# Trading an output quarter with two filter units in the batch plan, and ending on ScalarE's stores alone

## The chip, the core and the metric

The kernel runs on one core of one Trainium2 chip. TensorE (PE in the profile) multiplies, VectorE (DVE) and ScalarE (ACT) work on its results, GpSimd (POOL) and SyncE (SP) mostly start transfers; ACT can start them too. The metric is the device time of one execution in microseconds (us). A lower time is better.

## The reference

Two independent branches are computed from two inputs of shape 2048 x 448 and written side by side.

```python
q = (x @ wq).reshape(B, S, H, Dh).transpose(0, 2, 1, 3)   # H = 16 heads of Dh = 28
k = x @ wk                                                # one key and one value head for all
v = x @ wv
p = softmax(einsum("bhqd,bkd->bhqk", q, k) * Dh ** -0.5)
a = einsum("bhqk,bkd->bhqd", p, v).transpose(0, 2, 1, 3).reshape(B, S, H * Dh) @ wo
X = rfft2(B_x, axes=(-2, -1)) * (w_r + 1j * w_i)          # S x (D//2+1) spectrum
b = irfft2(X, s=(S, D), axes=(-2, -1))
out = concatenate([a, b], axis=-1)
```

## The kernel before

**Start.** Queries, keys and values are projected on TensorE, and the first stage of the Fourier filter runs beside that.

**Middle.** The attention is cut into 256 steps. A step is one of 16 blocks of 128 keys, against one chunk `c` of 512 rows and one group `g` of four heads; step number = 16 * (4c + g) + key block. Each step has four score products (line 917, 128x512, one per head), four exponentials on ACT (line 852, or a copy by DVE on line 923 and a later exponential in place, line 942), and then 16 products with the values (line 863). Results of products lie in eight PSUM banks (`s0` to `s5`, `sx`, `po`), and a score product needs a bank that ACT or DVE has emptied.

Steps go in batches. A table `PLAN` has one string for each batch, written out by `spread(n, units, ...)`: `n` steps, whose scores come first (`-`: exponential by ACT at once; `k`: copied by DVE first), with units of other work set between them; after the scores come the products with the values of the whole batch. I count batches from 0 by their place in `PLAN`. The letters are:

- `X` stands for four `W`s, `wo_unit(c, k, 0..3)`: the output projection of one block `k` of 128 rows of chunk `c`, over all four groups (11 products on line 771), then a copy by DVE and a store. I call an `X` an output quarter, since four make a chunk.
- `Z` is one filter unit of the last Fourier stage. For each of eight pieces `q` there are four: `fft3_a(q, 0)`, `fft3_a(q, 1)` (line 675), `fft3_b(q, 0)`, `fft3_b(q, 1)` (lines 699 to 701). `ZZ` is two units.

Which quarter or which unit comes at a letter is only the next in its list, so the letters' order decides it. Loads that a unit needs (`c2` on SP, line 666, and `fi` on POOL, line 668) are placed by the step of their first unit; the queues of SP, POOL, ACT, DVE and PE each work in order.

A finished pair (c, g) is divided by its sums on DVE, split into a coarse part `oh` and a rest `ol`, and then `spares(c, g)` copies rows of `ol` into unused rows of `oh` (SP, line 732, four transfers) and of `ol` (POOL, line 735, four transfers). An output quarter of chunk `c` reads them for every `g`.

**End.** The last chunk's projection is not in the plan. Behind the last products with the values, for its four row blocks k = 0 to 3, `partial(k)` multiplies the first three groups (nine products) and `final(k)` the last group (three products, lines 968 to 970) and stores the block with `wo_out`. The stored tile `yb` has two buffers: blocks 0 and 2 share one, and blocks 1 and 3 share the other, so the copy of block 3 waits until block 1's store has landed.

After that each engine reads a word `bits` (line 994) and branches on it (line 995). The branch leads past a large exact version of the attention, which these inputs don't take. SP then waits for the semaphores of all transfers, and a barrier of all engines ends the program (line 1181, which stands for the program's end).

Of the kernel before, what the change touches and what calls it, by code (L numbers as in the profile page):

```python
# [14 lines left out]
AF = mybir.ActivationFunctionType  # L15
# [5 lines left out]
S, D, H = 2048, 448, 16  # L21
# [16 lines left out]
def spread(n, units, lazy=4, start=0.9, rest=0.85, apart=1.0):  # L38

    late = 8 if lazy > 4 else 4  # L40
    m = 4 * n - late
    out = [(float(i), "-") for i in range(m)]
    out += [(apart * j + 0.5 if j < lazy else m + 0.1 * j, "k" if j < lazy else "e") for j in range(late)]
    out += [(m * (j + start) / (len(units) + rest) - 0.4, u) for j, u in enumerate(units)]
    return "".join(k for _, k in sorted(out)).replace("X", "WWWW").replace("Y", "ZZ")


PLAN = ["eeee"] + ["eeeeF"] + [spread(2, "", 0, 1.05)] + 2 * [spread(2, "", 0)] + [spread(5, "A", 4, 1.6)]
# [10 lines left out]
PLAN += [spread(7, "X", 8, 0.6, 0.35, 1.5)] + [spread(7, "ZZZ", 8, 0.9, 0.6, 1.5)]  # L59
PLAN += [spread(7, "Z", 8, 0.45, 0.6, 2.0)] + [spread(7, "ZZZ", 8, 0.9, 0.97, 2.5)]  # L60
PLAN += [spread(7, "ZZZ", 8, 0.9, 0.6, 2.0)] + [spread(8, "ZZZ", 7, 0.9, 0.6, 2.0)]
PLAN += [spread(7, "X", 8, 0.6, 0.6, 2.0)] + [spread(6, "X", 8, 0.9, 0.6, 2.0)]
PLAN += [spread(7, "ZZ", 8, 0.9, 0.6, 1.75)] + [spread(7, "X", 8, 0.9, 0.6, 2.25)]
PLAN += [spread(7, "X", 8, 0.6, 0.6, 1.5)] + [spread(7, "ZZZ", 8, 0.6, 0.6, 2.0)]
PLAN += [spread(7, "ZZ", 8, 0.9, 0.6, 2.0)] + [spread(7, "ZZ", 8, 0.6, 0.85, 2.0)]

# [5 lines left out]
def kernel(ctx: ExitStack, tc: tile.TileContext, t: dict):  # L72
    nc = tc.nc
# [73 lines left out]
    def fft1_a_mm(q, p):  # L147
        f, cs1 = ff[q], fc["cs1"][:113]
        pa = pair_of(bank())
        for e in range(2):  # L150
            for k, (n, o0) in enumerate(((113, 0), (112, 113))):
                for h in range(2):
                    for r in range(2):
                        r0 = 64 * h + 32 * r
                        mm(pa[r0:r0 + 32, e, o0:o0 + n], f[:, 2 * r + k, 2 * p + e, h], cs1[:, 2 * r + k, :n],  # L155
                           start=True, stop=True)
        return pa

    def fft1_a_out(q, p, pa):
        a = at1[q, p] = fp.tile([128, 2, DF], F32, name="a", tag=("pwr", "pwi")[p])  # L160
        return nc.scalar.activation(a, pa, AF.Copy)

    def fft1_b(q):
        return fft1_out(q, fft1_mm(q))
# [92 lines left out]
    with tc.tile_pool(name="w1", bufs=1) as w1:  # L257
# [37 lines left out]
        with tc.tile_pool(name="x1", bufs=2) as x1:  # L295
# [63 lines left out]
            def evac(c, g, pq):  # L359
                cs = slice(c * CW, (c + 1) * CW)  # L360
                out = nc.scalar.activation(qraw[:, g, cs], pq, AF.Copy)
                nc.vector.tensor_reduce(qmx[:, g, c:c + 1], qraw[:, g, cs], axis=AX.X, op=ALU.max,
                                        apply_absolute_value=True)
                return out
# [55 lines left out]
            for c in range(1, NC):  # L420
                for g in range(NG):
# [3 lines left out]
                    last = evac(c, g, pq)  # L425
# [43 lines left out]
        for p in range(2):  # L469
            last = fft1_a_out(6, p, fft1_a_mm(6, p))  # L470
# [7 lines left out]
        last = fft1_b(5)  # L478
# [26 lines left out]
    d, f, a, b, e, c = free  # L505
# [6 lines left out]
    def take():  # L512
        ready, bank = free.pop(free.index(min(free, key=lambda x: x[0])))
        clock["pe"] = max(clock["pe"], ready + 100)
        return bank
# [32 lines left out]
    def at_once(work=640, engine="dve"):  # L548
        clock[engine] = max(clock[engine], clock["pe"] + 200) + work
# [215 lines left out]
    def wo_mm(p, c, k, gs):  # L765
        s = slice(k * 128, k * 128 + 128)
        for g in gs:
            for n, (x, w) in enumerate(((oh, woh[:, g]), (ol, wox[:, g - 1] if g else woh[:, 0]), (oh, wol[:, g]))):
                if n == 1 and g == 0 and c < NC - 1:
                    continue  # L770
                mm(p, x[c][:, g, s], w, start=(g == 0 and n == 0), stop=(g == NG - 1 and n == 2))  # L771

    def wo_out(p, c, k, last=0):
        y = pp.tile([128, D], F32, name="yb", tag=f"p{k % 2}") if last else ap.tile([128, D], F32, name="ya")
        r0 = c * CW + k * 128
        for e in ((0, 1) if last == 4 else (0,)):
            s = slice(e * D // 2, (e + 1) * D // 2) if last == 4 else slice(0, D)
            if last and not e:
                nc.scalar.activation(y[:, s], p[:, s], AF.Copy)
            else:  # L780
                nc.vector.tensor_copy(y[:, s], p[:, s])
                at_once()
            (nc.scalar if last == 4 and not e else nc.sync).dma_start(t["oa"][r0:r0 + 128, s], y[:, s])

    wps = {}

    def wo_unit(c, k, g):
        if g == 0:
            wps[c, k] = take()
        p = wps[c, k][:, :D]  # L790
        need(("o", c, g))
        for x in (g,) if g == 0 else (g, g + NG - 1):
            need(("wo", x))
        wo_mm(p, c, k, (g,))
        passed(600 if g else 400)
        if g == NG - 1:
            wo_out(p, c, k)
            give(wps.pop((c, k)))
# [95 lines left out]
    for tokens in PLAN:  # L894
# [10 lines left out]
        for k in tokens:  # L905
# [9 lines left out]
            c, g, kc = steps[i if kind == "-" else n - 1 - i]  # L915
# [21 lines left out]
        for i in reversed(range(stay)):  # L937
# [5 lines left out]
            else:  # L943
                for h in hs:
                    p = keep[i][h // 2][:, h % 2]
# [12 lines left out]
    c = NC - 1  # L958
    ws = []

    def partial(k):
        ws.append(take()[:, :D])
        wo_mm(ws[k], c, k, range(NG - 1))

    def final(k):
        p, s = ws[k], slice(128 * k, 128 * k + 128)
        h, l = oh[c][:, NG - 1, s], ol[c][:, NG - 1, s]
        mm(p, h, woh[:, NG - 1], start=False, stop=False)
        mm(p, l, wox[:, NG - 2], start=False, stop=False)
        mm(p, h, wol[:, NG - 1], start=False, stop=True)  # L970
        wo_out(p, c, k, k + 1)


    flush(kept)
# [1 line left out]
    for k in range(4):  # L976
        divide(c, NG - 1, k)
        s = slice(128 * k, 128 * k + 128)
# [3 lines left out]
        nc.vector.tensor_tensor(ol[c][:, NG - 1, s], on[:, s], h.bitcast(F32), op=ALU.subtract)  # L982
    for k in (0, 1):
        partial(k)
    for k in (2, 3):
        final(k - 2)
        partial(k)
    final(2)
    final(3)


# [3 lines left out]
    with tc.If(rv > int(np.float32(BOUND).view(np.int32))), tc.tile_pool(name="g1", bufs=1) as g1:  # L995
# [32 lines left out]
        oa = t["oa"].rearrange("(n p) d -> n p d", p=128)  # L1028
        with tc.For_i(0, NC, 1) as nq:
            y = g1.tile([128, 4, D], F32, name="y")  # L1030
            nc.vector.memset(y, 0.0)
            with tc.For_i(0, NG, 1) as ng:
# [5 lines left out]
                for i in range(4):  # L1038
# [3 lines left out]
                    with tc.For_i(0, 16, 1) as nk:  # L1042
# [5 lines left out]
                        p = g1.tile([128, CW], F32, name="pe")  # L1048
# [136 lines left out]
```

## Time and profile before

| | |
|---|---|
| median of 3 runs | 640.84 us (639.79 to 642.42) |
| profiled execution | 640.64 us, its span 638.9 us |
| busy: PE, ACT, DVE, POOL | 628.8, 547.0, 440.8, 61.1 us |
| granted TensorE clock | 0.997 of full speed |
| batch 38 (steps 201 to 207) | from 500.65 to 518.03 us of the span |
| batch 39 (steps 208 to 213) | 518.03 to 531.26 |
| batch 40 (steps 214 to 220) | 531.26 to 546.01 |
| last products with values end, end stage begins | 621.79 |

The span goes from the first to the last instruction of the program; 1.74 us of the profiled execution lie outside it. Positions in the text are us from the span's start. "PE busy" is no measure of speed, since products overlap in the pipeline; how far apart the starts of products lie is one.

### The profile page before, as it was taken

What the parts mean: (1) busy time and instruction counts of PE and PEld (TensorE: products, weight loads), DVE (VectorE), ACT (ScalarE), POOL (GpSimd) and SP (SyncE); (2) the same over time, 40 slices, a digit from 0 to 9 for tenths busy, and PEclk for the clock granted to TensorE, in tenths of its full rate; (3) what the DMA queues carried; (4) which work ended last, traced back from release to release, by engine and by line L of the source; (5) the groups of instructions that cost most, each with busy time, mean ns of one, the idle gap of its engine ahead of it and who ended that gap; (6) DMA issues with size and microseconds to landing.
All of it is one profiled execution on the core that took longest, in us unless ns stands there. A gap on an engine that the chain in (4) does not pass through costs nothing.

```text
span 638.9 us, 12167 instructions
## 1 busy us (share of the span) xinstructions
PE 628.8 (98%) x4442; PEld 378.3 (59%) x4442; DVE 440.8 (69%) x793; ACT 547.0 (86%) x983; POOL 61.1 (10%) x118
## 2 busy tenths in 40 slices
PE   9999999999999999999999999999999899999995
PEld 7877645656555556646555665555556555555554
DVE  5999648889998934856766845386687446476652
ACT  5654999999999998988999989899989799889881
POOL 3021401011202110001110100001010100000000
PEclk9999999999999999999999999999999999999998
DMA  8855963456454613125340503044331404120011
GB/s 276 267 167 154 263 177 87 114 145 184 114 158 114 154 48 82 60 71 178 83 114 9 136 16 81 15 103 127 80 87 38 120 18 109 39 69 30 2 30 61
DMA packets 37459, 66.74 MB, mean 104 GB/s; under 512 B 7961, under 2 KB 21930, under 8 KB 36428
## 3 DMA queue, kind: packets, MB, share of 16 engines
q1 hardware_dynamic: 32608, 53.31, 30.1%
q0 software_dynamic: 4640, 12.48, 7.5%
q8 instruction: 36, 0.59, 0.4%
q14 instruction: 31, 0.25, 0.1%
q10 hardware_dynamic: 144, 0.11, 0.1%
HBM read 29.81 MB, written 17.87 MB: 75 GB/s over the span
## 4 chain that ended last, share of the span: by engine, by line
PE 96%; DMA 1%; SPq 1%; DVE 0%; issue 0%; ACT 0%; ACTq 0%; DVEq 0%
PE s L863 30%; PE s L917 28%; PE s L357 6%; PE sx L917 5%; PE po L917 5%; PE po L863 4%; PE s L771 4%; PE s L155 2%; PE sx L771 1%; PE s L675 1%; PE pbb L174 1%; PE s L572 1%; PE s L573 1%; PE s L574 1%; PE sx L675 1%; PE s L305 1%
## 5 line engine op out<-in xcount | busy, mean ns | idle before, releaser
L852 ACT ACTIVATE p<-s 128x512 f32<-128x512 f32 x410 | 223.7, 637 | 28.7 <-PE s L917 28.0
L917 PE MATMUL s<-qa,ka 128*128 128x512 f32 x751 | 226.6, 403 | 0.0
L917 PEld LDWEIGHTS s<-qa,ka 128*128 128x128 f32 x751 | 137.2, 188 | 62.1 <-issue 27.7
L863 PE MATMUL s<-p,vs 128*32 128x512 f32 x1040 | 129.7, 595 | 0.0
L923 DVE COPY k<-s 128x512 f32<-128x512 f32 x116 | 76.4, 685 | 56.8 <-PE s L917 56.5
L852 ACT ACTIVATE qraw<-s 128x512 f32<-128x512 f32 x138 | 79.2, 654 | 5.0 <-PE s L917 4.9
L942 ACT ACTIVATE k<-k 128x1024 f32<-128x1024 f32 x80 | 83.5, 1143 | 0.0
L863 PEld LDWEIGHTS s<-p,vs 128*32 128x32 f32 x1040 | 31.4, 109 | 68.5 <-issue 63.3
L917 PE MATMUL sx<-qa,ka 128*128 128x512 f32 x143 | 57.4, 401 | 0.0
L863 PE MATMUL s<-qraw,vs 128*32 128x512 f32 x432 | 55.4, 593 | 0.0
L917 PE MATMUL po<-qa,ka 128*128 128x512 f32 x130 | 52.6, 405 | 0.0
L852 ACT ACTIVATE p<-po 128x512 f32<-128x512 f32 x74 | 47.1, 637 | 4.5 <-PE po L917 4.2
L852 ACT ACTIVATE p<-sx 128x512 f32<-128x512 f32 x60 | 38.6, 644 | 3.9 <-PE sx L917 3.8
L863 PE MATMUL s<-k,vs 128*32 128x512 f32 x320 | 41.8, 594 | 0.0
L735 POOL DMA_DIRECT2D ol<-ol x36 | 18.0, 508 | 230.5 <-DVE ol L758 153.3
L917 PEld LDWEIGHTS sx<-qa,ka 128*128 128x128 f32 x143 | 26.9, 188 | 10.3 <-issue 4.2
L863 PEld LDWEIGHTS s<-qraw,vs 128*32 128x32 f32 x432 | 13.5, 110 | 30.8 <-issue 29.0
L867 DVE STREAM_TRANSPOSE osb<-s 128x512 f32<-128x512 f32 x14 | 10.0, 716 | 31.2 <-PE s L863 31.1
L917 PEld LDWEIGHTS po<-qa,ka 128*128 128x128 f32 x130 | 24.4, 188 | 10.8 <-issue 5.0
L923 DVE COPY k<-sx 128x512 f32<-128x512 f32 x27 | 18.5, 684 | 13.0 <-PE sx L917 13.0
L923 DVE COPY k<-po 128x512 f32<-128x512 f32 x17 | 11.6, 685 | 21.5 <-PE po L917 21.4
L852 ACT ACTIVATE qraw<-sx 128x512 f32<-128x512 f32 x34 | 21.8, 640 | 2.6 <-PE sx L917 2.6
(280 smaller groups left out, 964.8 us busy)
## 6 DMA issues: line engine op xcount, KB each, us to landing
qa<-qa SPq DMA_DIRECT2D x15, 512.0 KB
raw<-xa SPq DMA_DIRECT2D x16, 256.0 KB
xb<-xb SPq DMA_DIRECT2D x8, 512.0 KB
qa<-qh SPq DMA_DIRECT2D x64, 64.0 KB
qa<-ql SPq DMA_DIRECT2D x60, 64.0 KB
t<-bs SPq DMA_DIRECT2D x16, 225.0 KB
wr<-wr POOLq DMA_DIRECT2D x16, 225.0 KB, 3.9
wi<-wi POOLq DMA_DIRECT2D x16, 225.0 KB, 5.3
```

The costliest lines, as they stand in the source:

```text
L155: mm(pa[r0:r0 + 32, e, o0:o0 + n], f[:, 2 * r + k, 2 * p + e, h], cs1[:, 2 * r + k, :n], start=True, stop=True)
L174: mm(pb[h][64 * e:64 * e + 64, p], w[64 * h:64 * h + 64, 2 * p + e], a[64 * h:64 * h + 64, e], start=True, stop=True)
L357: mm(pq, w[:, j, gs], x[:, j], start=(j == 0 and n == 0), stop=(j == 3 and n == 1))
L675: mm(pz[:w, j], c2["c", q][:, j, o0:o0 + w], c2["F", q][:, j], start=True, stop=True)
L735: nc.gpsimd.dma_start(ol[c][o, g].bitcast(F32), ol[c][r, 0].bitcast(F32))
L771: mm(p, x[c][:, g, s], w, start=(g == 0 and n == 0), stop=(g == NG - 1 and n == 2))
L852: nc.scalar.activation(tiles[-1][:, h % 2], sc, AF.Exp, scale=SCALE)
L863: mm(po[c, g][32 * i:32 * i + 32], vs[:, kc], ps[i // 2][:, i % 2], start=(n == 1), stop=(n == 16))
L867: nc.vector.transpose(o, po[c, g])
L917: begun.append(mm(sc, ka[:, kc * 128:(kc + 1) * 128], qa[c, g][:, h], start=True, stop=True))
L923: nc.vector.tensor_copy(keep[i][h // 2][:, h % 2], sc)
L942: nc.scalar.activation(p, p, AF.Exp, scale=SCALE)
```

## The change

There are three edits. In `PLAN`, batch 38 had an output quarter and batch 40 two filter units; they trade places (the pacing numbers go with them). In `wo_out`, block 3 of the last chunk was cut in two halves, one copied and stored by ACT and the other copied by DVE and stored by SP, and blocks 0 to 2 were copied by ACT and stored by SP; now all four are copied whole by ACT, and stored by ACT. In the end stage, `partial(3)` came ahead of `final(2)` and now comes behind it.

```diff
-PLAN += [spread(7, "X", 8, 0.6, 0.6, 2.0)] + [spread(6, "X", 8, 0.9, 0.6, 2.0)]
-PLAN += [spread(7, "ZZ", 8, 0.9, 0.6, 1.75)] + [spread(7, "X", 8, 0.9, 0.6, 2.25)]
+PLAN += [spread(7, "ZZ", 8, 0.9, 0.6, 1.75)] + [spread(6, "X", 8, 0.9, 0.6, 2.0)]
+PLAN += [spread(7, "X", 8, 0.6, 0.6, 2.0)] + [spread(7, "X", 8, 0.9, 0.6, 2.25)]
...
-    def wo_out(p, c, k, last=0):
+    def wo_out(p, c, k, last=False):
...
-        for e in ((0, 1) if last == 4 else (0,)):
-            s = slice(e * D // 2, (e + 1) * D // 2) if last == 4 else slice(0, D)
-            if last and not e:
-                nc.scalar.activation(y[:, s], p[:, s], AF.Copy)
-            else:
-                nc.vector.tensor_copy(y[:, s], p[:, s])
-                at_once()
-            (nc.scalar if last == 4 and not e else nc.sync).dma_start(t["oa"][r0:r0 + 128, s], y[:, s])
+        if last:
+            nc.scalar.activation(y, p, AF.Copy)
+        else:
+            nc.vector.tensor_copy(y, p)
+            at_once()
+        (nc.scalar if last else nc.sync).dma_start(t["oa"][r0:r0 + 128], y)
...
-        wo_out(p, c, k, k + 1)
+        wo_out(p, c, k, True)
...
-    for k in (2, 3):
-        final(k - 2)
-        partial(k)
+    final(0)
+    partial(2)
+    final(1)
     final(2)
+    partial(3)
     final(3)
```

Line numbers behind `wo_out` fall by two in the changed kernel (917 becomes 915, 994 becomes 993, and so on).

On PE, in the middle of batch 38's scores, there stand before (`s4` is a bank, `woh`, `wol`, `wox` are parts of the output weights, `qa` queries, `ka` keys):

```order
L917 MATMUL s5_90<-qa_4457,ka_67 128x512
L917 MATMUL s3_88<-qa_4457,ka_67 128x512
L771 MATMUL s4_89<-woh_1059,oh_4144 128x448
L771 MATMUL s4_89<-wol_1060,oh_4144 128x448
L771 MATMUL s4_89<-woh_1059,oh_4144 128x448
L771 MATMUL s4_89<-wox_1061,ol_4145 128x448
```

In the changed kernel, at the same place on PE, with `c2` and `zh` the data of piece q = 5:

```order
L915 MATMUL s5_90<-qa_4457,ka_67 128x512
L699 MATMUL s3_88<-c2_4626,cs3h_3122 113x256
L700 MATMUL s3_88<-c2_4626,cs3l_3123 113x256
L701 MATMUL s3_88<-zl_4802,cs3h_3122 113x256
L699 MATMUL s3_88<-zh_4774,cs3h_3122 113x256
```

The quarter that read `oh` and `ol` here now begins in batch 39, and the unit `fft3_b(5, 1)` stands in its place; `fft3_a(6, 0)` follows 12 scores later.

On SP, from the last four copies of `oh` on, in the order before (`qa_5043` are the queries of step 224 and on):

```order
L732 DMA oh_4144<-ol_4145 4x512 x3
L230 DMA qa_4762<-qa_4762 64x2048
L732 DMA oh_4144<-ol_4145 4x512
L783 DMA oa<-ya_4941 128x448
L228 DMA qa_5043<-qh_5041 32x512
```

And in the changed kernel, on SP from the same copies on, where `qa_5054` are those queries:

```order
L732 DMA oh_4144<-ol_4145 4x512 x3
L230 DMA qa_4762<-qa_4762 64x2048
L732 DMA oh_4144<-ol_4145 4x512
L666 DMA c2_5501<-t2_73 32x4x225 x3
L720 DMA ob<-yo_4946 112x512
L715 DMA ob<-y1_4941 112x512
L716 DMA oc<-y1_4941 1x512
L666 DMA c2_5501<-t2_73 32x4x225
L228 DMA qa_5054<-qh_5052 32x512
```

The load of `c2` for piece 7 and the stores of piece 5's results now stand ahead of those queries' copies.

SP's end before, from the last store of the filter on:

```order
L716 DMA oc<-y1_5779 1x512
L783 DMA oa<-yb_5891 128x448
L783 DMA oa<-yb_5906 128x448
L783 DMA oa<-yb_5921 128x448
L783 DMA oa<-yb_5927 128x224
L994 TENSOR_LOAD bits_70
L995 COMPARE_AND_BRANCH
```

SP's end in the changed kernel:

```order
L720 DMA ob<-yo_5784 112x512
L715 DMA ob<-y1_5779 112x512
L716 DMA oc<-y1_5779 1x512
L993 TENSOR_LOAD bits_70
L994 COMPARE_AND_BRANCH
```

SP's four stores are gone, so that its word and its branch follow the filter's last store; on ACT the four copies now alternate with four stores, ahead of ACT's own word and branch.

## The prediction

> **What bounds the kernel now.** I began with the page's busy times and its chain of work that ended last.
>
> ```profile
> span 638.9 us, 12167 instructions
> PE 628.8 (98%) x4442; PEld 378.3 (59%) x4442; DVE 440.8 (69%) x793; ACT 547.0 (86%) x983; POOL 61.1 (10%) x118
> PE 96%; DMA 1%; SPq 1%; DVE 0%; issue 0%; ACT 0%; ACTq 0%; DVEq 0%
> ```
>
> TensorE sets the time nearly everywhere, so only what makes PE stand, or what comes behind its last product, can be won. The view of waits, for PE alone, has two rows; this is the one that lies in the middle, and the chain names its transfer:
>
> ```profile
> PE s L771 <- DMA oh<-ol: 1.8, 1, 1.8
> 502.30 4.72 DMA oh<-ol
> ```
>
> The timeline shows the place, first PE, then SP, which issues the transfer:
>
> ```profile
> 504.94 0.37 PE L771 MATMUL s<-wol,oh 128*128 128x448 f32 x1
> 507.16 0.45 PE L771 MATMUL s<-woh,oh 128*128 128x448 f32 x1 [1.84 <-DMA oh<-ol]
> 499.64 1.92 SPq L732 DMA_DIRECT2D oh<-ol  x3
> 502.30 0.59 SPq L732 DMA_DIRECT2D oh<-ol  x1
> ```
>
> This is batch 38. Its output quarter is chunk 2's first and needs the last pair's rows in `oh`; the fourth transfer is issued at 502.3 and lands 4.7 later, while PE already stands in front of the quarter's last three products. The next product should have started 0.2 after 504.94 and starts 2.2 after, so PE loses 2.0.
>
> Behind PE's last product there are 7 us more. The timeline gives PE's end and ACT's copies, the view by line the branch and what follows it, and SP's waits name the longest standstill there (the duration columns are minimum/median/maximum in ns, then first and last start):
>
> ```profile
> 631.40 0.36 PE L970 MATMUL po<-wol,oh 128*128 128x448 f32 x1
> 631.24 0.55 ACT L779 ACTIVATE yb<-s 128x448 f32<-128x448 f32 x1 [1.87 <-PE s L970]
> 632.34 0.36 ACT L779 ACTIVATE yb<-po 128x224 f32<-128x224 f32 x1 [0.56 <-DMA oa<-yb]
> 632.73 0.39 DVE yb L781
> L783 SPq DMA_DIRECT2D oa<-yb x4: 333/342/350, 627.0 to 633.2; - x4
> L994 SPq TENSOR_LOAD <-bits x1: 495/495/495, 633.5 to 633.5; - x1
> L995 SPq COMPARE_BRANCH  x1: 50/50/50, 634.1 to 634.1; - x1
> SPq L995 <- SPq L995: 2.6, 1, 2.6
> L995 SPq EVENT_SEMAPHORE  x6: 17/17/17, 636.8 to 637.2; - x6
> L1181 SPq EVENT_SEMAPHORE  x14: 17/28/28, 637.2 to 638.8; - x14
> L1181 POOLq EVENT_SEMAPHORE  x4: 17/17/17, 638.1 to 638.8; - x4
> ```
>
> SP issues its last store at 633.2, reads the word at 633.5, branches at 634.1, and goes on only at 636.8, released by nothing but itself. Then it walks through its list of semaphores and the barrier until 638.8. Were the last store's landing what counts, SP would be waiting for it; the transfers' bytes say otherwise. This is the DMA view from 629 to 636, in 40 slices of 0.175:
>
> ```profile
> GB/s 0 0 0 94 0 0 0 317 348 420 154 10 10 10 20 21 0 0 0 0 72 348 430 379 82 0 159 369 215 374 242 0 47 0 47 0 0 0 0 0
> 629.39 2.85 DMA oa<-yb
> ```
>
> The last stored bytes pass in the 31st slice, before 634.5. So SP's own standstill after the branch, and not the stores, sets the end.
>
> **Edit 1, batches 38 and 40.** No work is added or removed; the question is what each batch loses in its new place. Time of each batch's scores part, from the view by windows (length first, then busy time and count by engine), batches 38 to 42 in order:
>
> ```profile
> 500.65:511.89 11.24, 9.39 (x44) 7.14 (x40) 5.92 (x9) 7.55 (x16) 0.21 (x1) 1.00 0.41 119
> 518.03:525.97 7.94, 7.94 (x39) 6.42 (x35) 7.09 (x12) 6.54 (x15) 0.00 (x0) 1.00 0.11 26
> 531.26:539.87 8.61, 8.61 (x47) 6.54 (x43) 7.25 (x13) 8.07 (x18) 0.00 (x0) 1.00 0.42 99
> 546.01:555.13 9.12, 9.12 (x43) 7.09 (x39) 5.81 (x9) 7.91 (x16) 0.00 (x0) 1.00 0.07 26
> 561.28:570.15 8.87, 8.87 (x43) 7.21 (x39) 6.33 (x12) 7.14 (x15) 0.00 (x0) 1.00 0.42 100
> ```
>
> A seven-step batch with a quarter takes 8.87 to 9.12 when nothing is late; batch 38 takes 11.24, that is 2.1 to 2.4 more. With two units such a batch takes 8.61. Changed, the two sevens should take 8.61 in place 38 and 8.87 to 9.12 in place 40: 17.5 to 17.7 against 19.85 now, a gain of 2.1 to 2.4. Batch 39 comes behind a batch that no longer gave ACT and DVE 2 us of rest, and I give back 0.2 for that (a quarter behind two units is 0.25 over the quarter behind a quarter: 9.12 against 8.87). **Taken: 2.0.** Bounds: 2.4, and 0.3 if the stall only moves.
>
> The cover must hold for what moved. The quarter's rows land at 507.0 and are now read in batch 39, not before 515: 8 us of room. `fft3_a(6, 0)` moves from batch 40 to the second half of batch 38's scores, near 505; its `c2` pieces are issued with the rows of 470 to 480, and its `fi` stands before the last `ol` copies on POOL instead of behind them:
>
> ```profile
> 480.24 0.33 SPq L666 DMA_DIRECT2D c<-t  x1
> 469.62 0.57 POOL L668 DMA_DIRECT2D fi<-fi  x1
> 497.79 1.99 POOL L735 DMA_DIRECT2D ol<-ol  x4 [27.59 <-DVE ol L758]
> ```
>
> With POOL idle for 27 us ahead of those copies, `fi` goes out then, and costs nothing; were it issued only behind them (499.8) it would still come at about the time it is read. The `ol` copies may be 0.6 later, one `fi` issue, which has the same 8 us of room.
>
> **Edits 2 and 3, the end.** PE's products are the same; `final(2)` comes nine products earlier, `final(3)` stays last, so PE still ends at 631.76. ACT copies blocks 0 and 1 when it does now, block 2 earlier, since its products come earlier, and block 3 as now: the row at 632.34 shows that it waits for block 1's store, whose transfer took 2.85 to land, since a few of its packets dragged on until 631.8 (the slices of 10 to 21 GB/s). That store is issued at the same moment, so I keep 632.34. The copy is whole now: 0.55 by the row at 631.24, to 632.89, and the store is issued at once. Its landing is not shown; block 2's store, issued when its copy ended at 631.79, has its bytes through at about 633.3, and block 1's landed 0.4 behind its last bytes. So I estimate 1.9 to 2.0 from issue to landing: 634.85.
>
> SP has no store to issue any more. Its word and branch follow the filter's last store:
>
> ```profile
> 616.53 0.30 SPq L716 DMA_DIRECT2D oc<-y  x1
> L995 ACTq COMPARE_BRANCH  x1: 54/54/54, 633.7 to 633.7; - x1
> L995 ACTq EVENT_SEMAPHORE  x1: 17/17/17, 634.2 to 634.2; - x1
> L995 DVEq COMPARE_BRANCH  x1: 72/72/72, 633.4 to 633.4; - x1
> L995 DVEq EVENT_SEMAPHORE  x1: 21/21/21, 636.2 to 636.2; - x1
> ```
>
> SP's 2.6 then lies near 620, under PE's products, and so does DVE's 2.8 (DVE has no half block to copy either). ACT is the last to branch, 0.2 later than now, and went on after 0.5. So what comes late next is the landing of the last store at 634.85, and then what is left of SP's list and the barrier: all of it is 2.1 (636.8 to 638.8), the barrier alone 0.75 (638.1 to 638.8). Where the last store's semaphore stands in the list is not shown; I take 1.2, nearer the middle, and get 636.05 against 638.85. **Taken: 2.8.** Bounds: 1.9 and 3.2 by the list; 3.7 if block 1's store doesn't drag; 0.3 if only an issue is saved.
>
> The Trainium skill, "Runtime: NRT & Kernel Launch", section "Instruction fetch mechanics", says that a taken branch to a target outside the two pages held forces a fetch before the engine goes on. The trace agrees in kind: SP stands 2.6 and DVE 2.8, and ACT's 0.5 looks like a target at hand. It states no price for this, so by it the sum is the one made here from the rows.
>
> The sum: 640.64 - 2.0 - 2.8 = 635.84 for an execution like the profiled one. The median of the runs stands 0.2 above that execution, so I say **636.0**. About 0.5% (3.2 us) is what a measurement of this kernel can tell from no change: faster is below 637.6, slower above 644.0.
>
> **The rivals.**
>
> *ACT stands after its branch.* Its code is three instructions longer and its branch is now the last. If its target isn't at hand, it loses what SP lost, 2.6, or DVE, 2.8: branch at 633.9, on at 636.6, and 0.1 and the barrier behind it, 637.45. The tail gains 1.4, the time is 637.4. Against it: ACT went on after 0.5 with nearly the same code. The rule of the Trainium skill's section named above would bring this about where the three added instructions push the target out of what ACT holds.
>
> *The stall only moves.* With the rest gone, ACT and DVE run short of banks in batches 38 to 40, and the region gains 0.3: 637.7. ACT's busy time speaks against it, 13.7 of batch 40's 14.75 and the same 13.7 of batch 38's 17.38:
>
> ```profile
> 500.65:518.03 17.38, 15.54 (x99) 8.86 (x95) 5.92 (x9) 13.70 (x24) 0.21 (x1) 1.00 0.26 77
> 531.26:546.01 14.75, 14.75 (x102) 8.25 (x98) 8.91 (x15) 13.70 (x25) 0.00 (x0) 1.00 0.35 90
> ```
>
> *Only an issue is saved.* SP's standstill is then bound to the last engine's arrival, not to its own stores, and comes as late as before; the end gains one issue of 0.33 (the median of SP's stores): 638.5. Against it, SP's waits name no other engine. The Trainium skill, "DMA: Bandwidth & Descriptors", section "Issuing engines are not separate DMA queues", speaks for it: starting transfers from another engine saves only the time of starting them.
>
> *SP stands, and the time gets longer.* SP now has the load for piece 7 and piece 5's three result stores ahead of the copies of the queries for step 224. It waited for such a result once for 27.3:
>
> ```profile
> SPq L720 <- DVE yo L719: 27.3, 1, 27.3
> 523.25 0.54 SPq L228 DMA_DIRECT2D qa<-qh  x1
> 529.79 0.50 SPq L230 DMA_DIRECT2D qa<-qa  x1
> ```
>
> These copies take 7.0 to issue and, as `oh`'s, some 4.7 to land; batch 41, which reads them, began at 546.0 and would begin some 2 earlier, near 544. SP must be free by 532; it gets stuck from about 503, so up to 29 costs nothing, and beyond it PE waits one for one. To end slower than now the stand must pass 29 by the 4.8 of the sum, 34; at 38 the time is 645. Against it, DVE's order has piece 5's results before batch 39's copies, so the stand should be 7.
>
> *Neither edit pays*: 640.3.
>
> **How the numbers follow.** The forecast has 0.60, with its own range 634.6 to 637.3. ACT's stand has 0.12, the moved stall 0.13, the saved issue 0.08, neither 0.04, the stuck SP 0.03. The range leaves out the last three and reaches to the others' bounds: 634.6 to 638.3. Faster is the forecast, most of ACT's stand and half of the moved stall, 0.75; slower the stuck SP, 0.03; the rest, 0.22, is the same.
>
> **What would show it.** Right: no PE wait of over 0.5 in batch 38 or on the quarters' line, batch 38's scores part at 8.4 to 8.8 and batch 40's at 8.8 to 9.2; SP's branch near 617 and its 2.6 there, ACT's next instruction 0.5 behind its branch, and the program's end 4 to 5 behind PE's last product instead of 7.1. Wrong: a PE wait in batches 38 to 41, an ACT or SP standstill of 2 us or more after 633, or a time above 638.3.

## The result, and the profile after

The changed kernel's median is 636.0 us (635.32 to 636.85, six runs), beside 641.45 us (639.79 to 643.37, six runs) of the kernel before on the same chip. The ratio is 0.9915, with an interval from 0.9894 to 0.9936: faster by 5.5 us (4.1 to 6.8). Its profiled execution took 635.32 us, with a span of 633.5. This is the head of its page:

```profile
span 633.5 us, 12165 instructions
PE 628.3 (99%) x4442; PEld 378.3 (60%) x4442; DVE 440.4 (70%) x792; ACT 547.0 (86%) x983; POOL 61.2 (10%) x118
```

PE does the same 4442 products in nearly the same busy time (628.3 beside 628.8), and the span is 5.3 shorter. The view of PE's waits has one row left, far from the change; the wait for `oh` is gone:

```profile
PE s L305 <- DVE idle L301: 1.1, 1, 1.1
```

The view by windows has the scores parts of batches 38 to 40, and then these three batches as a whole, of the changed kernel and below it of the kernel before (length, then busy time and count of PE, PEld, DVE, ACT, POOL, then the granted clock, the DMA engines' busy share and GB/s):

```profile
500.40:509.05 8.65, 8.65 (x47) 6.53 (x43) 7.26 (x13) 8.06 (x17) 0.00 (x0) 1.00 0.59 144
515.19:523.17 7.98, 7.98 (x40) 6.45 (x36) 7.05 (x12) 6.51 (x14) 0.00 (x0) 1.00 0.11 26
528.46:537.57 9.11, 9.11 (x43) 7.19 (x39) 5.91 (x9) 7.57 (x17) 0.00 (x0) 1.00 0.28 68
500.40:543.72 43.32, 43.32 (x281) 25.06 (x277) 23.16 (x37) 39.16 (x68) 0.00 (x0) 1.00 0.30 78
500.65:546.01 45.36, 43.52 (x280) 24.99 (x276) 23.21 (x37) 39.23 (x68) 0.21 (x1) 1.00 0.29 79
```

The three batches take 43.32 instead of 45.36: 2.04 less. Batch 38 gives 11.24 - 8.65 = 2.59, and batch 40, which now has the quarter, takes back 9.11 - 8.61 = 0.50. Batch 39 comes to 7.98, beside 7.94.

The end, in the timeline: PE's last product, and ACT's copies and stores (for blocks 0 and 1 their stores' rows only, then copy and store of blocks 2 and 3):

```profile
629.07 0.36 PE L968 MATMUL po<-wol,oh 128*128 128x448 f32 x1
624.64 0.38 ACTq L781 DMA_DIRECT2D oa<-yb  x1
627.01 0.34 ACTq L781 DMA_DIRECT2D oa<-yb  x1
627.45 0.54 ACT L777 ACTIVATE yb<-s 128x448 f32<-128x448 f32 x1 [0.47 <-PE s L968]
628.02 0.70 ACTq L781 DMA_DIRECT2D oa<-yb  x1
629.85 0.54 ACT L777 ACTIVATE yb<-po 128x448 f32<-128x448 f32 x1 [1.86 <-SPq L994]
630.42 0.34 ACTq L781 DMA_DIRECT2D oa<-yb  x1
```

The copy of block 3 at 629.85 is put down to SP, whose list passed the same semaphore at 629.78. What both had waited for is block 1's store, which landed at 629.77.

And by line, the branches of SP and ACT, what each does next, and the list of semaphores at the program's end (durations in ns, then first and last start):

```profile
L994 SPq COMPARE_BRANCH  x1: 50/50/50, 615.4 to 615.4; - x1
L994 SPq EVENT_SEMAPHORE  x6: 17/17/17, 626.6 to 630.1; - x6
L994 ACTq COMPARE_BRANCH  x1: 54/54/54, 631.4 to 631.4; - x1
L994 ACTq EVENT_SEMAPHORE  x1: 17/17/17, 631.8 to 631.8; - x1
L1180 SPq EVENT_SEMAPHORE  x14: 17/28/28, 630.2 to 633.5; - x14
SPq L1180 <- DMA oa<-yb: 1.8, 2, 1.6
```

The last row, from SP's waits, is what had to show: in its list SP now waits for a store. It branches at 615.4, under PE's products, and stands for nothing of its own at the end. The first of its six semaphores passes at 626.6, 1.96 behind the issue of block 0's store, so it waited for that store, and a standstill behind the branch is covered. Here are the transfers' bytes from 626.5 to 633.5, in slices of 0.175:

```profile
GB/s 0 0 0 47 94 0 0 72 369 379 358 72 10 10 20 133 420 369 359 51 47 0 0 0 0 0 0 236 451 369 256 0 0 47 0 0 0 0 0 0
```

Block 3's bytes pass in the 28th to 31st slice. The little burst in the 34th is a packet of code of 8 KB (queue q14, at 632.44) and no part of the store: each store's landing is recorded as 16 completions, and the last of block 3's comes at 632.33. The program ends 1.2 later. PE ends at 629.43 (the row's 629.07 and 0.36), and the span goes on for 4.11 behind it, beside 7.11 before: 3.0 less. With 2.04 of the batches that is 5.04; the other 0.3 is almost all a batch 38 that started 0.25 earlier, behind work that the change doesn't touch.

### The profile page after: what moved, and what is told of

It is laid out like the page before. It is cut to its first block, busy times and chain, and to the rows that moved or that the text cites. A ratio compares the mean times of both kernels' runs of the same rounds, so it can differ in the third digit from the quotient of the medians.

```text
span 633.5 us, 12165 instructions
## 1 busy us (share of the span) xinstructions
PE 628.3 (99%) x4442; PEld 378.3 (60%) x4442; DVE 440.4 (70%) x792; ACT 547.0 (86%) x983; POOL 61.2 (10%) x118
## 5 line engine op out<-in xcount | busy, mean ns | idle before, releaser
L921 DVE COPY k<-s 128x512 f32<-128x512 f32 x122 | 80.1, 685 | 62.9 <-PE s L915 62.8
L861 PE MATMUL s<-p,vs 128*32 128x512 f32 x976 | 121.3, 595 | 0.0
L861 PEld LDWEIGHTS s<-p,vs 128*32 128x32 f32 x976 | 29.4, 109 | 64.3 <-issue 59.4
L915 PE MATMUL sx<-qa,ka 128*128 128x512 f32 x137 | 55.3, 404 | 0.0
L861 PE MATMUL s<-qraw,vs 128*32 128x512 f32 x384 | 49.5, 593 | 0.0
L850 ACT ACTIVATE p<-sx 128x512 f32<-128x512 f32 x64 | 41.5, 649 | 3.0 <-PE sx L915 2.9
L861 PE MATMUL s<-k,vs 128*32 128x512 f32 x304 | 39.7, 594 | 0.0
L861 PEld LDWEIGHTS s<-qraw,vs 128*32 128x32 f32 x384 | 12.0, 110 | 27.3 <-issue 26.1
L921 DVE COPY p<-s 128x512 f32<-128x512 f32 x35 | 23.0, 683 | 0.0
```

Of the source, the lines that this page charges most:

```text
L850: nc.scalar.activation(tiles[-1][:, h % 2], sc, AF.Exp, scale=SCALE)
L861: mm(po[c, g][32 * i:32 * i + 32], vs[:, kc], ps[i // 2][:, i % 2], start=(n == 1), stop=(n == 16))
L915: begun.append(mm(sc, ka[:, kc * 128:(kc + 1) * 128], qa[c, g][:, h], start=True, stop=True))
L921: nc.vector.tensor_copy(keep[i][h // 2][:, h % 2], sc)
```

## The experiments

In every one the kernel before ran on the same chip. Gains in time have the interval of the ratio; parts of a span are from one profiled execution.

**The trade of the plan alone.** The kernel before, with the two `PLAN` lines of the change and nothing else.

```diff
-PLAN += [spread(7, "X", 8, 0.6, 0.6, 2.0)] + [spread(6, "X", 8, 0.9, 0.6, 2.0)]
-PLAN += [spread(7, "ZZ", 8, 0.9, 0.6, 1.75)] + [spread(7, "X", 8, 0.9, 0.6, 2.25)]
+PLAN += [spread(7, "ZZ", 8, 0.9, 0.6, 1.75)] + [spread(6, "X", 8, 0.9, 0.6, 2.0)]
+PLAN += [spread(7, "X", 8, 0.6, 0.6, 2.0)] + [spread(7, "X", 8, 0.9, 0.6, 2.25)]
```

> The kernel before with the plan's trade alone. Theory (the quarter met its late rows in batch 38, and nothing takes that wait's place): no wait of PE in batches 38 to 41, batch 38's scores part 8.65, the batches 38 to 40 together 2.0 us shorter, the end still 7.1 us behind PE's last product, the span 636.8. Rival (the stall only moves): a new wait or gaps in batches 38 to 41, the span 638.5.

Median 639.03 beside 640.94; ratio 0.9966 (0.9953 to 0.9978), 2.2 us faster. By its windows, the three batches, and by line SP's end:

```profile
501.03:544.35 43.32, 43.32 (x280) 25.07 (x277) 23.13 (x37) 39.16 (x68) 0.00 (x0) 1.00 0.30 77
L995 SPq COMPARE_BRANCH  x1: 50/50/50, 632.5 to 632.5; - x1
L995 SPq EVENT_SEMAPHORE  x6: 17/17/17, 635.2 to 635.6; - x6
```

The batches take the 43.32 of the changed kernel, PE has no wait in batches 38 to 41, and SP still stands from 632.5 to 635.2 at the end. The trade's gain is whole by itself. The span of this execution, 637.3, is 0.5 over what was expected: batch 38 began 0.4 later than before, and the end took 7.25 behind PE's last product (630.09) and not 7.1.

**ScalarE's stores alone.** The kernel before with the new `wo_out`; plan and order of the products stay.

```diff
-        for e in ((0, 1) if last == 4 else (0,)):
...
-            (nc.scalar if last == 4 and not e else nc.sync).dma_start(t["oa"][r0:r0 + 128, s], y[:, s])
+        if last:
+            nc.scalar.activation(y, p, AF.Copy)
...
+        (nc.scalar if last else nc.sync).dma_start(t["oa"][r0:r0 + 128], y)
```

> The kernel before with the last four blocks copied and stored by ACT alone; the plan and the order of the last products as before. Theory (SP's standstill behind its branch set the end): SP branches near 617, the program ends 4.0 to 4.5 us behind PE's last product instead of 7.1, the span 635.8 to 636.3, and PE still waits 1.8 in batch 38. Rival (only an issue is saved): the end 6.8 behind PE's last product, the span 638.5.

Median 637.88 beside 640.94; ratio 0.995 (0.9935 to 0.9965), 3.2 us faster. PE's last product, SP's end, and the three batches:

```profile
span 636.3 us, 12162 instructions
631.51 0.36 PE L968 MATMUL po<-wol,oh 128*128 128x448 f32 x1
L993 SPq COMPARE_BRANCH  x1: 50/50/50, 617.9 to 617.9; - x1
500.68:546.12 45.44, 43.52 (x280) 24.98 (x277) 23.21 (x37) 39.23 (x68) 0.20 (x1) 1.00 0.30 79
```

The span ends 4.40 behind PE's last product, and the batches are as slow as before. The two parts add up: 2.2 and 3.2 are 5.4, beside 5.5 for the whole change.

**The order of the products alone.** The kernel before with `partial(3)` behind `final(2)`.

```diff
-    for k in (2, 3):
-        final(k - 2)
-        partial(k)
+    final(0)
+    partial(2)
+    final(1)
     final(2)
+    partial(3)
     final(3)
```

> The kernel before with the fourth block's products moved back alone. Theory: block 2's copy and store come 1.5 to 1.9 us earlier and nothing waits for them, block 3's path stays, so the span is 638.9 within 0.3. Rival (block 2's store, late in front of block 3's, held up the end): the end 1 us or more closer to PE's last product, the span 637.9 or less.

Median 640.64 beside 640.94; ratio 0.9993 (0.9983 to 1.0002): no change that can be told. Block 2's copy came at 629.90, 1.8 earlier against PE's end, as expected. SP still branches late and stands for 2.7, and the span ends 7.4 behind PE's end at 632.24:

```profile
span 639.6 us, 12167 instructions
631.88 0.36 PE L970 MATMUL po<-wol,oh 128*128 128x448 f32 x1
L996 SPq COMPARE_BRANCH  x1: 50/50/50, 634.8 to 634.8; - x1
L996 SPq EVENT_SEMAPHORE  x6: 17/17/17, 637.5 to 637.9; - x6
```

This span is 0.7 over the 638.9 that was expected. Of that, 0.5 stands ahead of PE's end, and the rest is block 3's copy, which started 0.83 behind PE's end instead of 0.58, since block 1's store landed later (see the last section).

**One store back on SP.** This decides whether SP's late branch was the price, or the stores themselves. The changed kernel, with only block 3's store issued by SP again:

```diff
-        (nc.scalar if last else nc.sync).dma_start(t["oa"][r0:r0 + 128], y)
+        (nc.scalar if last and k < 3 else nc.sync).dma_start(t["oa"][r0:r0 + 128], y)
```

> The changed kernel with block 3's store issued by SP, the copies all on ACT. Theory (SP's standstill behind its branch): SP issues near 630.4, branches near 631.3, goes on 2.6 later and then walks its list, so the program ends near 636.0, 2.5 us later than the changed kernel's 633.5. Rival (issuing engines differ only by the issue itself): 633.5 to 633.9.

Median 638.63 beside 640.94; ratio 0.9966 (0.9956 to 0.9977), so 3.3 us of the change's 5.5 are lost again by the ratios. In the timeline and by line:

```profile
span 636.6 us, 12165 instructions
629.42 0.36 PE L968 MATMUL po<-wol,oh 128*128 128x448 f32 x1
630.78 0.36 SPq L781 DMA_DIRECT2D oa<-yb  x1
L994 SPq COMPARE_BRANCH  x1: 50/50/50, 631.8 to 631.8; - x1
L994 SPq EVENT_SEMAPHORE  x6: 17/17/17, 634.5 to 634.9; - x6
```

The same store, issued 1.0 behind PE's end as in the changed kernel (630.42 against 629.43 there), and the end comes 6.80 behind PE instead of 4.11. The store landed at 632.94, 3.16 behind PE, but SP stood for 2.65 behind its branch until 634.5 and then walked its list and the barrier for 2.1: SP's own path, and no longer the landing, ends last. The Trainium skill, "DMA: Bandwidth & Descriptors", section "Issuing engines are not separate DMA queues", says that starting transfers on several engines saves only the time of starting them. Of the transfer that roughly holds here: it landed 2.16 behind its issue, beside 1.91 in the changed kernel. Of the program's time it does not, since what the issuing engine has to do next, its branch, comes late with it, and the measured 2.7 (6.80 beside 4.11) decides.

**The three earlier stores back on SP.** The counterpart: ACT keeps only block 3's store.

```diff
-        (nc.scalar if last else nc.sync).dma_start(t["oa"][r0:r0 + 128], y)
+        (nc.scalar if last and k == 3 else nc.sync).dma_start(t["oa"][r0:r0 + 128], y)
```

> The changed kernel with the stores of blocks 0 to 2 issued by SP and block 3's by ACT. Theory (SP's standstill costs only what of it lies behind the last landing): SP's last issue near 628, its branch near 629, on 2.6 later at about 631.6, and then some 14 entries of its list ahead of the last store's semaphore, near 632.5 against its landing at 632.3: the span 633.5 to 633.9. Rival (SP's standstill costs wherever its last store stands in the end stage): 634.5 or more.

One run, 635.65 us, with a span of 633.9. The span alone misleads here, since this execution was 0.3 ahead of the changed kernel's when PE ended (629.11 beside 629.43):

```profile
628.74 0.37 PE L968 MATMUL po<-wol,oh 128*128 128x448 f32 x1
L994 SPq COMPARE_BRANCH  x1: 50/50/50, 629.0 to 629.0; - x1
L994 SPq EVENT_SEMAPHORE  x6: 17/17/17, 631.8 to 632.2; - x6
L1180 SPq EVENT_SEMAPHORE  x14: 17/28/28, 632.2 to 633.8; - x14
```

Behind PE the end takes 4.77, so moving these three stores costs 0.66: more than my theory had (0 to 0.4), less than the rival's price (1.0). SP's last issue took 0.97, its branch fell at 629.0, and from 631.8 it ran its whole list before the barrier. It came to the last store's semaphore at 632.67, and that store had landed at 631.98, so its own list and no longer the last landing sets the end. A late branch on SP costs only what sticks out behind the last store's landing; that much of the theory stands, its size was off, and one run can't say by how much elsewhere.

**A buffer for each block.** The prediction let block 3's copy wait for block 1's store. In the changed kernel each block gets its own tile:

```diff
-        y = pp.tile([128, D], F32, name="yb", tag=f"p{k % 2}") if last else ap.tile([128, D], F32, name="ya")
+        y = pp.tile([128, D], F32, name="yb", tag=f"p{k}") if last else ap.tile([128, D], F32, name="ya")
```

> The changed kernel with a tile of its own for each of the last four blocks, so that block 3's copy waits for no store. Theory (block 1's store, dragging on, is what holds block 3's copy): the copy starts 0.1 behind PE's last product instead of 0.4, and the span is 0.3 shorter, 633.2. Rival (ACT is held by its own issues or the landing doesn't follow): no change, 633.5.

Median 635.79 beside 640.9; ratio 0.992 (0.9903 to 0.9936). Against the changed kernel (0.9915, 0.9894 to 0.9936) nothing can be told apart. Its timeline, ACT's last rows:

```profile
628.38 1.04 ACTq L781 DMA_DIRECT2D oa<-yb  x1
629.88 0.54 ACT L777 ACTIVATE yb<-po 128x448 f32<-128x448 f32 x1 [1.53 <-PE po L968]
630.46 0.34 ACTq L781 DMA_DIRECT2D oa<-yb  x1
```

The copy waits for PE now and starts 0.04 behind PE's end instead of 0.42. That half of the theory holds. The gain of 0.4 did not come: the end is 4.14 behind PE. Block 3's store landed 2.93 behind PE, as in the changed kernel (2.90), although it was issued 0.4 earlier against PE's end. The trace shows where that went. From 630.06 to 630.92 a packet of 8 KB of code ran, in the midst of block 2's store. The DMA view from 630.0 to 631.0 has it (packets, MB, share of 16 engines):

```profile
q14 instruction: 1, 0.01, 5.4%
```

Of block 2's 16 completions, 15 came by 631.02 and the last at 632.25, 1.33 behind that packet. Of block 3's, 15 came by 632.36 and the last at 632.77. So the 0.4 that the copy saved came back as a drag of the last store. No run shows this kernel without the packet.

**The last rows copied by POOL.** Is it the plan's trade that matters, or only that the rows came late? The kernel before, in which the four copies into `oh` of pair (2, 3) are issued by POOL instead of SP, where eight copies of queries stand ahead of them:

```diff
-            nc.sync.dma_start(oh[c][o, g].bitcast(F32), ol[c][r, 0].bitcast(F32))
+            eng = nc.gpsimd if (c, g) == (2, 3) else nc.sync
+            eng.dma_start(oh[c][o, g].bitcast(F32), ol[c][r, 0].bitcast(F32))
```

> The kernel before, its plan untouched, with the four transfers into oh of the one pair that batch 38's quarter waits for issued by POOL instead of SP, where eight copies of queries stand ahead of them. Theory (the wait is SP's queue, and PE's time is free once the rows are there): POOL issues the last of them near 501.7, they land near 504, PE doesn't wait in batch 38, and the span is 2.0 shorter, 636.9, as with the trade. Rival (the trade pays by giving ACT and DVE a better balance): the wait goes, but gaps in batches 38 to 40 take over 1 us of it back.

Median 639.2 beside 640.9; ratio 0.9976 (0.9965 to 0.9986), 1.5 us faster (0.9 to 2.2), where 2.0 were expected. Batch 38's scores part, the three batches, and the last copy's issue:

```profile
500.41:509.53 9.12, 9.12 (x44) 7.19 (x40) 5.91 (x9) 7.56 (x16) 2.21 (x5) 1.00 0.51 148
500.41:543.66 43.25, 43.25 (x280) 25.05 (x276) 23.19 (x37) 39.21 (x68) 2.21 (x5) 1.00 0.31 83
500.53 0.50 POOL L733 DMA_DIRECT2D oh<-ol  x1
```

Issued at 500.53 instead of 502.3, the rows are in time, and the quarter in its old place costs nothing: 43.25 beside the trade's 43.32. So the trade gains because it gets out of the way of a late transfer, not because its order is better for the other engines. It is a second way to the same 2 us. The two were not run together, but the changed kernel has no PE wait left in batch 38 that the second could remove.

**PE's branch later.** The drag of block 1's store goes with a transfer of code behind PE's branch (shown below). The changed kernel, with ten further small products behind `final(3)` whose result nothing reads, so that PE branches later:

```diff
     final(3)
+    spent = take()[:, :128]
+    for _ in range(10):
+        mm(spent, woh[:, 0, :128], woh[:, 0, :128], start=True, stop=True)
```

> The changed kernel with ten further 128x128 products on PE behind the last block's, whose result nothing reads, so that PE's sequencer comes to its branch, and to the 16 KB of code fetched there, some 1 to 2 us later. In eight traces the code packet starts 2.1 us ahead of PE's last product, and block 1's store lands 1.4 us behind that packet's end, whatever its length (0.93 to 1.39). Theory (the code packet holds one of the transfer engines, and block 1's last packets stand behind it): block 1's store lands by 0.4 us ahead of the last block's last product instead of 0.3 behind it, block 3's copy starts 0.1 behind that product instead of 0.4, and the end is 4.1 behind it or up to 0.3 less, as long as the packet doesn't meet block 3's store. Rival (the store drags for its own place in the stage): block 1 lands 0.3 behind, as before.

Median 635.36 beside 640.55; ratio 0.9921 (0.9904 to 0.9938). PE's last product of a block, PE's branch (PEldq is PE's sequencer), ACT's store of block 2 and its last copy, and the bytes from 626.7 to 633.5 in slices of 0.17:

```profile
629.31 0.36 PE L968 MATMUL po<-wol,oh 128*128 128x448 f32 x1
L997 PEldq COMPARE_BRANCH  x1: 358/358/358, 628.8 to 628.8; - x1
628.27 0.34 ACTq L781 DMA_DIRECT2D oa<-yb  x1
629.71 0.54 ACT L777 ACTIVATE yb<-po 128x448 f32<-128x448 f32 x1 [1.47 <-PE po L968]
GB/s 0 0 0 0 48 0 0 0 253 443 369 274 11 0 274 432 369 274 145 0 0 0 0 0 0 0 337 390 411 211 0 0 48 0 0 0 0 0 0 0
```

PE's branch, at 626.2 in the changed kernel, came at 628.8, and the code packet behind it at 629.85 instead of 627.34. Block 1's store passes in the 9th to 12th slice with almost no drag behind it. It landed 0.48 ahead of that product's end, where in the changed kernel it landed 0.34 behind; the copy starts at +0.04, and the end is 3.84 behind instead of 4.11. The mechanism holds. In the time, 0.3 is too little to be told from the changed kernel, so this is no version that is shown to be better.

## Why the prediction was right, point by point

**What bounds the kernel.** PE's one wait in batch 38 and SP's standstill at the end were the two places, and both are shown by experiments: the rows copied earlier give the first back without the trade, and one store returned to SP brings the second back without anything else.

**Edit 1, taken 2.0, measured 2.04.** Batch 38 came to 8.65 (forecast 8.4 to 8.8) and batch 40 to 9.11 (8.8 to 9.2). The rest is a small miss: batch 39 gave back 0.04 instead of 0.2, and batch 40 was at the top of its bounds, so the two errors cancel. The stall did not only move: no PE wait stands in batches 38 to 41. The cover held, by SP's waits from 495 to 535 and its timeline:

```profile
SPq L720 <- DVE yo L719: 3.9, 1, 3.9
520.40 0.55 SPq L228 DMA_DIRECT2D qa<-qh  x1
```

SP stood for piece 5's result for 3.9, where the prediction said 7 and feared over 29, and the queries' copies began at 520.4, 2.9 earlier than before. The wait of 27.3 that the prediction named as a warning lies elsewhere: SP stood there from 588.1 to 615.4, for the last piece's result, and it stands there for 27.4 now.

**Edits 2 and 3, taken 2.8, measured 3.0.** SP's branch went to 615.4 (near 617 was said, on the clock of the kernel before). The last store landed 1.91 behind its issue, 632.33 (1.9 to 2.0 was estimated), and 1.2 followed (1.2). That second agreement is luck: the prediction had no row for the store's place in SP's list and took a value near the middle. The term that was mis-sized is the wait of block 3's copy for block 1's store: I kept it as before, 0.58 behind PE's end (632.34 against 631.76), and it was 0.42. Its size goes with how long a packet of code happens to take (last section), so it was no constant of the kernel. The order of the products, which I counted at nothing by itself, gave nothing that can be told.

**The rivals.** ACT did not stand after its branch: 631.4 to 631.8, with three more instructions. Only an issue saved: the end gained 3.0, and SP's standstill left the end together with its stores. By the Trainium skill's rule on branches, "Runtime: NRT & Kernel Launch", section "Instruction fetch mechanics", an engine must fetch a target that it doesn't hold before it goes on. SP's 2.7 wherever its branch is late agrees; that ACT's 0.5 means a target at hand is a reading that no run tested.

**The total.** 636.0 forecast, 636.0 measured: that is closer than the working deserves. The gain did not come out as closely: the forecast has 4.8, and the ratio says 5.5. The kernel before stood at 641.45 in the runs beside the changed one and at 640.84 in those of the forecast, and that hides the difference. The sum was made for an execution of 640.64 and came to 635.84; the profiled one took 635.32, of which 0.25 is an earlier start of batch 38 and most of the rest the end's 0.2.

## What to carry to other kernels

The last store's issuer matters less for the transfer than for what that engine must still do: give the last stores to an engine whose way to the program's end is short, and let the others branch early, under work. A transfer that comes late can be cured in two ways, by reading it later or by issuing it from a queue where less stands ahead of it; look which of the two is free. And measure an end from the last product of the busiest engine, not from the span, since the start differs by half a microsecond between executions.

## What the runs showed of the hardware that I had not expected

**Code shares the way with data.** About 2.1 ahead of PE's end, and 1.1 behind PE's branch in each of these kernels, one packet of 16 KB of instructions passes among the DMA packets. Its rows, from the DMA view over the 2 us that end 0.2 ahead of PE's end, for the kernel before, the changed kernel and the kernel with the products' order alone (packets, MB, share of 16 engines):

```profile
q8 instruction: 1, 0.02, 3.7%
q8 instruction: 1, 0.02, 3.2%
q8 instruction: 1, 0.02, 4.3%
```

Of 32 us of engine time these shares are 1.18, 1.02 and 1.38 us for one packet. Block 1's store is under way at the same time. In the kernel before, 15 of its 16 completions came by 0.43 ahead of PE's end, and the last alone 0.48 behind it. The packet's own length and that last completion, for every kernel in which the packet came there:

| kernel | code packet, us | block 1 landed behind PE's end, us |
|---|---|---|
| three stores on SP | 0.93 | 0.25 |
| changed | 1.01 | 0.34 |
| last store on SP | 1.02 | 0.35 |
| rows on POOL | 1.05 | 0.36 |
| before | 1.17 | 0.48 |
| plan alone | 1.29 | 0.59 |
| own buffers | 1.31 | 0.62 |
| stores alone | 1.32 | 0.62 |
| order alone | 1.39 | 0.72 |

The store lands 1.40 to 1.42 behind that packet's end in each, and when PE's branch, and with it the packet, came later, the store was in time. That the packet and the store's last part share one DMA engine fits this, but the traces don't name the engine.

**An issue is not always 0.35.** A store's issue on ACT or SP took 0.33 to 0.38 in the end stage, but block 2's took 0.70 in the changed kernel, 0.71 with the last store on SP, 0.97 with three stores on SP, 1.04 with own buffers and 1.45 with the order alone. In these five it came 0.6 to 1.0 behind block 1's issue, while that store and the code packet were both under way, and in each it ended 0.36 to 0.38 behind the packet's end. Another store under way is not enough: with PE's branch later, block 2's store came 1.0 behind block 1's as well, without the packet, and took 0.34. Why the issue waits for the packet is not shown.

**The price of the branch belongs to the engine.** From the branch's start to the next instruction SP took 2.65 to 2.78 where that could be seen, DVE 2.8 to 3.0, and ACT 0.47 each time. Why ACT's is short no run shows.
